# Attention and a multiplicative FFN on one core: the attention part on two 64-row tiles of TensorE instead of one of 128 rows

## The chip, the core and the metric

The kernel runs on one core of a Trainium2 chip. The metric is device time in microseconds (us). In the profile the engines are PE (TensorE matmuls), PEld (its weight loads), DVE (VectorE), ACT (ScalarE), POOL (GpSimd) and SP (which only issues DMAs). Results of TensorE land in PSUM, which the kernel uses as eight banks of 512 float32 columns on 128 partitions.

## What is computed

Attention over 8 batches of 8 heads, with queries pooled in pairs, and then a feed-forward part on the 4608 resulting rows:

```python
# q, k, v: 8 x 8 x 1152 x 64
q_pool = q.reshape(B, H, S // 2, 2, D).mean(axis=3)          # 576 queries per head
scores = scale * np.matmul(q_pool, k.transpose(0, 1, 3, 2))  # 576 x 1152
attn = exp(scores - max) / sum
attn_out = np.matmul(attn, v)
x = attn_out.transpose(0, 2, 1, 3).reshape(4608, 512)
a = x @ w1; b = x @ w2                                       # 512 x 1024 each
h = a * b @ w3                                               # 1024 x 1024
out = h @ w_out                                              # 1024 x 512
```

The kernel multiplies w3 and w_out first (`T16`), so that a row needs w1, w2 and `T16`.

## The kernel before

**Pairs of heads.** Two heads form a pair `p`; there are 32 pairs, four per batch. For each pair k and q come by DMA, POOL casts and pools them into `kq16` (`cast_kq`), and they are transposed into `kqT`: on TensorE for pairs 1 to 7 (`transp_pe`, L323), by DMA from pair 8 on (`transp`). Head 0 of a pair lies on partitions 0 to 63 and head 1 on 64 to 127.

**Slots.** The scores of all pairs are one long strip of columns, cut into 324 slots of 512. A slot (`scores`, L379) is one or two pieces per head, each a matmul of 64 rows; the two heads write two banks of a `psc` buffer, of which there are three. One exponential on ACT (L393) empties a slot into `ring`, which holds 24 x 576 columns, or 2.67 pairs.

**Attention times V.** A pair has five tiles of 128 queries (the last one overlaps, since 576 is not a multiple). A group `av_pair(i)` (L406) is one tile for both heads: 18 matmuls of 128 rows and 65 columns, 64 of V and a constant column that gives the sum. Three column ranges of one bank, `avb`, take turns. DVE takes the reciprocal of the sums and multiplies (`av_norm`, L429); `x_turn` (L443) and `x_copy` (L450) turn the result into `xT`, or from pair 8 on a DMA does (`x_dma`).

**Fill.** The feed-forward part is cut into groups that fill TensorE's time between slots: first the w3 transposes and `T16` (`t_groups`, L467), then for each chunk of 512 rows (`moe_groups`, L522) sixteen projection groups (w1 and w2 in turn, four matmuls of 128 rows and 512 columns each, L506) and four output groups (eight such matmuls, L550). DVE empties a group's bank: a copy `asb` (L535), then a multiplication into `gT` (L539), or a scaled copy `osb` (L560), which is stored. A group's bank is `mo`, of which there is one, or half of a `psc` buffer (`bank`, L462). There are nine chunks. A chunk is handed out when its last attention tile is done, later ones five groups afterwards (`HELD`).

**Order.** The program is written out in visits (from L685). A visit puts out three slots and then a string of pair transposes, attention groups and fill groups that a planner picks:

```python
due = max(due + PACE, plan.t + 2.6)      # PACE = 3.09 for three slots
...
for what in plan.visit(due, ...):        # up to six pieces: P, A, m, s
```

`_Plan` (L122) holds a cost in microseconds for every piece, 0.09 for a change between 64 and 128 rows among them, and the time at which ACT and DVE give each buffer back. `visit` tries the possible strings and takes the cheapest. The planner's times only set the order; on the chip every instruction waits on semaphores for its buffers. After the last slot the rest of the fill runs without attention (the tail): the `psc` buffers take turns there, and ACT takes part of the evacuations.

Of the kernel before, what the change touches and what calls it, by code (L numbers as in the profile page):

```python
# [121 lines left out]
class _Plan:  # L122
# [3 lines left out]
    SWITCH, SLOT, AV, TURN, PAIR, SEEN = 0.09, 0.222, 0.553, 0.055, 0.76, 0.05  # L126
    STEP = {0.5: 0.45, 1: 0.866, 2: 1.73}

    def __init__(self, t):
        self.t = t  # L130
        self.act = self.mo = self.av = self.dve = 0.0
        self.psc = [0.0, 0.0, 0.0]
        self.k = 0
        self.row = True

    def _pe(self, row, free, took):
        if row != self.row:
            self.t += self.SWITCH
            self.row = row
        self.t = max(self.t, free) + took  # L140

    def _psc(self):
        self.k += 1
        return (self.k - 1) % 3

    def scores(self):
        b = self._psc()
        self._pe(True, self.psc[b] + self.SEEN, self.SLOT)
        self.act = max(self.act, self.t + 0.21) + 0.953
        self.psc[b] = self.act + 0.07  # L150

    def fill(self, n, at, scored):
        b = self._psc() if scored else None
        self._pe(False, max(at, (self.psc[b] if scored else self.mo) + self.SEEN), self.STEP[n])
        self.dve = max(self.dve, self.t + 0.2) + 0.69
        if scored:
            self.psc[b] = self.dve + 0.07
        else:
            self.mo = self.dve + 0.07

    def av_group(self, turns):
        self._pe(False, self.av + self.SEEN, self.AV + (self.TURN if turns else 0.0))
        self.dve = max(self.dve, self.t + 0.2) + 0.49 + (0.21 if turns else 0.0)
        self.av = self.dve + 0.02

    def pair(self, at):
        b = self._psc()
        self._pe(False, max(at, self.psc[b] + self.SEEN), self.PAIR)
        self.dve = max(self.dve, self.t + 0.1) + 0.9
        self.psc[b] = self.dve + 0.07  # L170

    def copy(self):
        p = _Plan(self.t)
        p.__dict__.update(self.__dict__)
        p.psc = list(self.psc)
        return p

    def visit(self, due, turns, must, groups, pair_at, eager):


        best = [None, None]

        def end(p, seq, work, av):
            q = p.copy()
            for _ in range(3):
                q.scores()
            lost = q.t - self.t - work - 3 * self.SLOT
            cost = lost + 0.2 * abs(p.t - due) + 0.3 * max(q.av + self.SEEN - q.t, 0.0)
            cost -= eager * min(len(turns), 6) * av
            if best[0] is None or cost < best[0] - 1e-9:  # L190
                best[:] = [cost, seq]

        def step(p, seq, work, av, f, pr):
            if pr == len(pair_at) and av >= must:
                end(p, seq, work, av)
            if len(seq) > 5 or p.t > due + 0.5 and av >= must:
                return
            if pr < len(pair_at):
                q = p.copy()
                q.pair(pair_at[pr])  # L200
                step(q, seq + "P", work + self.PAIR, av, f, pr + 1)
            if av < min(len(turns), 3):
                q = p.copy()
                q.av_group(turns[av])
                step(q, seq + "A", work + self.AV + (self.TURN if turns[av] else 0.0), av + 1, f, pr)
            if f < min(len(groups), 4):
                n, at = groups[f]
                for b in (False, True):
                    q = p.copy()
                    q.fill(n, at, b)  # L210
                    step(q, seq + "ms"[b], work + self.STEP[n], av, f + 1, pr)

        step(self, "", 0.0, 0, 0, 0)
        return best[1]


@with_exitstack
def kernel(
# [53 lines left out]
    avb = ps.tile([128, 512], FP32, tag="av", bufs=1)  # L272
    xpt = avb.bitcast(FP16)[:, 896:1024]
    xps = avb[:, 448:448 + QT]
# [48 lines left out]
    def transp_pe(p):  # L323
        kq16 = pairs[p]
        kqT = att.tile([128, NB, 128], FP16, tag="kqT", bufs=3)
        pt = ps.tile([128, 2, 512], FP32, tag="psc", bufs=3, name="ptk").rearrange("p b c -> p (b c)").bitcast(FP16)
        for n, c in enumerate(range(NB - 1, -1, -1)):
            nc.tensor.transpose(pt[:, c * 128:c * 128 + 128], kq16[:, c].rearrange("p u d -> p (u d)"), ident16)  # L328
        for c0, c1 in ((8, NB), (0, 4), (4, 8)):
            nc.vector.tensor_copy(out=kqT[:, c0:c1].rearrange("p c i -> p (c i)"), in_=pt[:, c0 * 128:c1 * 128])  # L330
        pairs[p] = kq_views(kqT)
# [43 lines left out]
    def turn_bank():  # L375
        return ps.tile([128, 512], FP32, tag="mo", bufs=1, name="ptf").bitcast(FP16)


    def scores(s):  # L379
        psc = ps.tile([128, 2, 512], FP32, tag="psc", bufs=3, name="psc")  # L380
# [25 lines left out]
    def av_pair(i):  # L406
        p, t = i // NT5, i % NT5
        va = vaugs[p % NVA]
        o = (i % 3) * 2 * E1
        for jt in range(NJ):  # L410
            c0 = ((p * NJ + jt) * Sq) % RING + TO[t]
            for u in range(2):
                nc.tensor.matmul(avb[:, o + u * E1:o + u * E1 + E1], ring[:, u, c0:c0 + 128], va[:, u, jt, :],  # L413
                                 start=(jt == 0 and u == 0), stop=(jt == NJ - 1), skip_group_check=True)

    XD = 8
    xb5 = {}

# [7 lines left out]
    def on_pe(i):  # L426
        return i >= 0 and (i // NT5 < XD or i % NT5 == QM)

    def av_norm(i):  # L429
        av = avb[:, (i % 3) * 2 * E1:(i % 3) * 2 * E1 + 2 * E1].rearrange("p (u e) -> p u e", e=E1)  # L430
        nc.vector.reciprocal(out=rzall[:, i, :], in_=av[:, :, D:E1].rearrange("p u o -> p (u o)"))  # L431
        p, t = i // NT5, i % NT5
        if on_pe(i):
            xbt = att.tile([128, 2, D], FP16, tag="xbt", bufs=3)
        else:
            if t == 0:
                xb5[p] = att.tile([128, QM, 2, D], FP16, tag="xb5", bufs=3, name="xb5")
            xbt = xb5[p][:, t]
        nc.vector.tensor_tensor(out=xbt, in0=av[:, :, 0:D],
                                in1=rzall[:, i, :].unsqueeze(2).to_broadcast([128, 2, D]), op=ALU.mult)  # L440
        xbts[i] = xbt

    def x_turn(i):  # L443
        xb = xbts.pop(i).rearrange("p u d -> p (u d)")
        if i % NT5 < QM:
            nc.tensor.transpose(xpt, xb, ident16)
        else:
            nc.tensor.matmul(xps, xb, ident16[:, 128 - QT:128], start=True, stop=True, skip_group_check=True)
# [142 lines left out]
    def fill(scored=False):  # L591
# [7 lines left out]
        if put:  # L599
            put(pt)  # L600
# [196 lines left out]
```

## Time and profile before

| What | Value |
| --- | --- |
| time, median of two runs | 422.69 us (421.59 and 423.79) |
| profiled execution | 421.38 us, its span 419.4 us |
| granted TensorE clock | 1.000 |
| 64-row score matmuls (L388) | 1152, mean 290 ns |
| 128-row attention matmuls (L413) | 2880, mean 193 ns |
| exponentials (L393) | 324, 308.1 us in all, the last one ends at 349.2 us |
| first projection matmul (L506) | starts at 67.2 us |
| HBM read and written | 67.11 and 9.44 MB |

A group's row names line, engine and operation, what is written from what, shapes and count; then its busy time in us, the mean of one in ns, and the idle time of the engine just ahead of it with what ended that. A row of stretches gives, for a window of the span, the busy time and the number of instructions of each engine. A row of the timeline gives start and length in us of instructions that follow one another.

### The profile page before, as it was taken

To read this page: it belongs to the slowest core of one execution; us is meant where nothing else is said; L and a number is where in the kernel's file an instruction comes from. 1 tells how busy PE (TensorE), PEld (TensorE's weight loads), DVE (VectorE), ACT (ScalarE), POOL (GpSimd) and SP (SyncE) were. 2 spreads that over 40 slices of the span, in tenths; PEclk is the share of its full clock that TensorE was granted. 3 is DMA by queue.
4 is the path that set the end of the run, shared out by engine and by line. 5 is a ranking of instruction groups with operands and counts; after the bars stand their busy time and mean duration, and the time that the engine had idled before them with its cause. 6 is when DMAs were issued, how large, how long until landed. Compare 5 with 4: busy or idle time off the path is not lost.

```text
span 419.4 us, 12782 instructions
## 1 busy us (share of the span) xinstructions
PE 406.3 (97%) x5337; PEld 253.2 (60%) x5337; DVE 204.8 (49%) x601; ACT 326.4 (78%) x359; POOL 165.7 (40%) x206
## 2 busy tenths in 40 slices
PE   4899999999999999999999999999999999999995
PEld 2588786566565656665566656666577756444442
DVE  1255666655355545455355534554454546624231
ACT  4888979899899989998899889999899882223231
POOL 5889967360573317250664318340642011000000
PEclk9999999999999999999999999999999999999999
DMA  8999999999798898999979999998896214020203
GB/s 273 265 305 294 287 299 325 279 264 199 188 253 208 234 262 223 272 279 265 251 195 262 253 240 291 209 266 227 225 217 120 56 64 64 14 101 2 100 0 106
DMA packets 90960, 86.34 MB, mean 206 GB/s; under 512 B 59664, under 2 KB 64272, under 8 KB 90896
## 3 DMA queue, kind: packets, MB, share of 16 engines
q1 hardware_dynamic: 81600, 59.32, 58.0%
q0 software_dynamic: 8720, 25.10, 20.6%
q10 hardware_dynamic: 576, 1.05, 0.8%
q8 instruction: 42, 0.69, 0.7%
q14 instruction: 22, 0.18, 0.2%
HBM read 67.11 MB, written 9.44 MB: 183 GB/s over the span
## 4 chain that ended last, share of the span: by engine, by line
PE 94%; ACT 2%; DVE 1%; DMA 1%; issue 1%; POOL 0%; ACTq 0%; POOLq 0%
PE avb L413 22%; PE psc L388 20%; PE mot L506 15%; PE mo L506 15%; PE mo L550 10%; PE mot L550 5%; PE mo L484 3%; ACT ring L393 2%; PE ptk L328 2%; DMA kst<-in_k_dram 1%; PE mot L484 1%; PE mot L475 1%; PE mo L475 1%; DVE kqT L330 1%; PE mol L568 0%
## 5 line engine op out<-in xcount | busy, mean ns | idle before, releaser
L393 ACT ACTIVATE ring<-psc 128x1024 f16<-128x1024 f32 x324 | 308.1, 1025 | 34.4 <-PE psc L388 32.6
L413 PEld LDWEIGHTS <-ring 128*128 128x128 f16 x2880 | 103.6, 98 | 32.1 <-issue 10.4
L413 PE MATMUL avb<-vaug,ring 128*128 128x65 f16 x2880 | 114.4, 193 | 0.1
L388 PE MATMUL psc<-kqT 64*128 64x512 f16 (+7 forms) x1152 | 96.7, 290 | 3.2 <-ACT ring L393 1.0
L388 PEld LDWEIGHTS <-kqT 64*128 64x128 f16 x1152 | 45.6, 95 | 35.0 <-issue 12.3
L300 POOL CAST kq<-kst 128x1152 f16<-128x1152 f32 x31 | 35.7, 1151 | 73.5 <-DMA kqT<-kq 52.6
L431 DVE RECIPROCAL rzall<-avb 128x2 f32<-128x2 f32 x160 | 26.3, 164 | 55.8 <-PE avb L413 26.3
L550 PE MATMUL mo<-T,gT 128*128 128x512 f16 x192 | 45.5, 380 | 0.0
L506 PEld LDWEIGHTS <-w2sb 128*128 128x128 f16 x320 | 28.4, 97 | 26.6 <-issue 2.1
L518 POOL DMA_DIRECT2D out_dram<-osb x21 | 11.7, 555 | 81.0 <-DVE osb L560 45.1
L550 PEld LDWEIGHTS <-gT 128*128 128x128 f16 x280 | 25.5, 98 | 30.1 <-issue 2.9
L506 PEld LDWEIGHTS <-w1sb 128*128 128x128 f16 x320 | 27.9, 97 | 26.0 <-issue 3.6
L313 POOL CAST vaug<-vst 128x1152 f16<-128x1152 f32 x32 | 36.6, 1143 | 8.8 <-DMA vst<-in_v_dram 8.8
L304 POOL TENSOR_TENSOR kq<-qst 128x512 f16<-128x512 f32 x31 | 39.4, 1272 | 1.5 <-DMA qst<-in_q_dram 1.5
L506 PE MATMUL mot<-xT,w2sb 128*128 128x512 f16 x156 | 40.0, 379 | 0.0
L506 PE MATMUL mo<-xT,w1sb 128*128 128x512 f16 (+2 forms) x168 | 39.2, 359 | 0.0
L539 DVE TENSOR_TENSOR gT<-mot,asb 128x512 f16<-128x512 f32 x39 | 26.9, 691 | 23.6 <-PE mot L506 23.6
L535 DVE COPY asb<-mo 128x512 f32<-128x512 f32 x38 | 26.3, 691 | 23.8 <-PE mo L506 23.8
L560 DVE TENSOR_SCALAR osb<-mo 128x512 f32<-128x512 f32 x24 | 16.6, 691 | 39.2 <-PE mo L550 39.2
L533 ACT COPY asb<-mot 128x512 f32<-128x512 f32 x20 | 11.7, 585 | 30.4 <-PE mot L506 30.4
L506 PE MATMUL mot<-xT,w1sb 128*128 128x512 f16 (+2 forms) x152 | 34.9, 356 | 0.0
L506 PE MATMUL mo<-xT,w2sb 128*128 128x512 f16 (+2 forms) x164 | 34.0, 338 | 0.0
(69 smaller groups left out, 275.8 us busy)
## 6 DMA issues: line engine op xcount, KB each, us to landing
vst<-in_v_dram SPq DMA_DIRECT2D x25, 576.0 KB, 4.8
kst<-in_k_dram SPq DMA_DIRECT2D x23, 576.0 KB, 5.7
qst<-in_q_dram SPq DMA_DIRECT2D x23, 512.0 KB, 7.3
out_dram<-osb POOLq DMA_DIRECT2D x21, 256.0 KB, 5.9
kst<-in_k_dram POOLq DMA_DIRECT2D x8, 576.0 KB, 9.5
qst<-in_q_dram POOLq DMA_DIRECT2D x8, 512.0 KB, 10.5
vst<-in_v_dram POOLq DMA_DIRECT2D x7, 576.0 KB, 6.3
out_dram<-osb SPq DMA_DIRECT2D x9, 256.0 KB, 2.0
```

The lines of the kernel that those rows point to most:

```text
L300: nc.gpsimd.tensor_copy(out=kq16[:, 0:NJ].rearrange("p c u d -> p u c d"), in_=kst.rearrange("p u (c d) -> p u c d", d=D))
L304: eng.tensor_tensor(out=kq16[:, NJ:NJ + QM].rearrange("p c u d -> p u c d"), in0=qv[:, :, :, 0], in1=qv[:, :, :, 1], op=ALU.add)
L313: nc.gpsimd.tensor_copy(out=va[:, :, :, 0:D], in_=vs.pop(p).rearrange("p u (c d) -> p u c d", d=D))
L388: nc.tensor.matmul(psc[:, u, f - s * G:f - s * G + ln], kT2[u * 64:u * 64 + 64, jt, :], qpT[u * 64:u * 64 + 64, i0:i0 + ln], start=True, s ...
L393: nc.scalar.activation(out=ring[:, :, r0:r0 + G], in_=psc, func=AF.Exp, bias=0.0, scale=SCALE)
L413: nc.tensor.matmul(avb[:, o + u * E1:o + u * E1 + E1], ring[:, u, c0:c0 + 128], va[:, u, jt, :], start=(jt == 0 and u == 0), stop=(jt == N ...
L431: nc.vector.reciprocal(out=rzall[:, i, :], in_=av[:, :, D:E1].rearrange("p u o -> p (u o)"))
L484: nc.tensor.matmul(pT[:, 0:256], w3T[ft][:, a, :], wosb[:, a, n0:n0 + 256], start=(a == 0), stop=(a == NF - 1))
L506: nc.tensor.matmul(pw[:, d0:d0 + n], wt[:, mc, ft * 128:ft * 128 + 128], xT[:, mc, a:a + n], start=(mc == 0 and d0 == 0), stop=(mc == NC - ...
L535: nc.vector.tensor_copy(out=t["a"], in_=pa)
L539: nc.vector.tensor_tensor(out=t["g"][:, ft, :], in0=pb, in1=t["a"], op=ALU.mult)
L550: nc.tensor.matmul(po, t["g"][:, ft, tt:tt + 128], T16[:, ft, :], start=(ft == 0), stop=(ft == NF - 1))
```

## The change

**All on 64 rows.** Up to the last slot, every product of 128 rows becomes products of 64 rows that come in twos, the one on partitions 0 to 63 and the other on 64 to 127. Scores were that already. A unit (class `Unit`) makes two results at a time, in the two banks of `fb`: for a projection the w1 and the w2 result of one slice, for the output two tiles of 128 rows. In the first half of a unit, rows 0 to 63 add to result 0 and rows 64 to 127 to result 1; in the second half they swap. Between the halves stands a `mark`: a copy by DVE of one element of bank 1, which the second half's first matmul must wait for. A projection unit has two steps of eight matmuls of 64 rows and 512 columns, an output unit or a `T16` unit four. `fb` exists once; a unit's two evacuations on DVE come after its last step.

**Attention times V** is done for two tiles at a time (three groups per pair: tiles 0 and 1, 2 and 3, 4), the two heads in the two banks of `avt`, again in two halves with a mark between. `av_norm` handles both tiles at once. The transposes (`transp_pe`, `x_turn`, w3) are made of 64-row ones likewise.

**Buffers.** `psc` has two buffers of two banks instead of three, `fb` two banks instead of `mo`'s one, `avt` two instead of `avb`'s one.

**Order.** Visits and their search are gone. The program is written out piece by piece: of the pieces whose buffers are free by the plan, a slot goes first, then a pair transpose; of attention and fill, attention if it is behind its slots by more than a pair and else fill; if none is free, the one that will be first. A half does not follow its own first half directly. A slot is held back (`owed`) while the ring has no room. `PACE` is 1.01 per slot, `HELD` is 3. In the tail products are of 128 rows as before; three two-bank buffers take turns.

```diff
-    SWITCH, SLOT, AV, TURN, PAIR, SEEN = 0.09, 0.222, 0.553, 0.055, 0.76, 0.05
-    STEP = {0.5: 0.45, 1: 0.866, 2: 1.73}
+    SLOT, AV, STEP, TURN, KQ, SEEN = 0.226, 0.275, 0.866, 0.06, 0.45, 0.05
...
-    def visit(self, due, turns, must, groups, pair_at, eager):
...
-    avb = ps.tile([128, 512], FP32, tag="av", bufs=1)
+    avt = ps.tile([128, 2, 512], FP32, tag="av", bufs=1)
...
+    ROWS = (slice(0, 64), slice(64, 128))
+
+    def fill_banks():
+        return ps.tile([128, 2, 512], FP32, tag="fb", bufs=1, name="fb")
...
-        psc = ps.tile([128, 2, 512], FP32, tag="psc", bufs=3, name="psc")
+        psc = ps.tile([128, 2, 512], FP32, tag="psc", bufs=2, name="psc")
...
+    def mark(bank, c):
+
+        nc.vector.tensor_copy(out=scrap, in_=bank[0:1, c:c + 1])
+
+    def av_half(i, half):
+        for n, jt, c0, va in av_views(i):
+            for r in (0, 1):
+                u = r ^ half
+                nc.tensor.matmul(avt[:, u, n * E1:n * E1 + E1], ring[ROWS[r], u, c0:c0 + 128], va[ROWS[r], u, jt, :],
+                                 start=(half == 0 and n == 0 and jt == 0), stop=(jt == NJ - 1),
+                                 skip_group_check=True)
+        if not half:
+            mark(avt[:, 1, :], (len(BT[i % NBT]) - 1) * E1)
...
+        def step(self):
+            if self.q == 0:
+                self.pt = fill_banks()
+            if self.single:
+                self.single(self.pt)
+            else:
+                per = self.nk // 4
+                half, k0 = self.q // per, 4 * (self.q % per)
+                for kk in range(k0, k0 + 4):
+                    for r in (0, 1):
+                        j = r ^ half
+                        self.mm(self.pt[:, j, :], j, kk, ROWS[r], half == 0 and kk == 0,
+                                kk == self.nk - 1)
+                if self.q == per - 1:
+                    mark(self.pt[:, 1, :], 0)
+            self.q += 1
+            if self.q == len(self.costs):
+                self.put(self.pt)
...
+            def put(pt):
+                asb = msb.tile([128, CH], FP32, tag="asb", bufs=2, name="asb")
+                nc.vector.tensor_copy(out=asb, in_=pt[:, 0, :])
+                nc.vector.tensor_tensor(out=t["g"][:, ft, :], in0=pt[:, 1, :], in1=asb, op=ALU.mult)
...
-    PACE = 3.09
+    PACE = 1.01
...
+        owed = s < NS and avn[0] < NAB and frees(avn[0]) < s * G + G
...
+        if s < NS and not owed and not (turn_due and s >= turned * FLAT // G):
+            may["S"] = max(plan.scores_at(), due)
+        i = avn[0]
+        if ahalf[0]:
+            if last != "A":
+                may["A"] = swap_at["A"]
+        elif i < NAB and i // NBT in pair_exp and s < NS:
+            may["A"] = max(plan.av + plan.SEEN, pair_exp[i // NBT] + 0.1)
+        if unit:
+            if not (unit.swaps() and last == "F"):
+                may["F"] = swap_at["F"] if unit.swaps() else 0.0
+        elif turn_due:
+            may["P"] = max(plan.fb + plan.SEEN, KQ_AT.get(turned, 0.0))
+        elif head() and s < NS:
+            may["F"] = max(plan.fb + plan.SEEN, head().at)
...
+        now = [w for w in may if may[w] <= plan.t + 0.03]
+        if not now:
+            now = [min(may, key=lambda w: may[w])]
+        if "S" in now:
+            what = "S"
+        elif "P" in now:
+            what = "P"
+        elif "A" in now and "F" in now:
+
+            what = "A" if (i + 3) * FLAT + LAG * G < s * G * NBT else "F"
+        else:
+            what = now[0]
```

## The prediction

> **What bounds the kernel now.** I read the busy table and the chain of waits of the page first, then the costliest groups, then stretches of the span, and last TensorE's own timeline.
>
> ```profile
> PE 406.3 (97%) x5337; PEld 253.2 (60%) x5337; DVE 204.8 (49%) x601; ACT 326.4 (78%) x359; POOL 165.7 (40%) x206
> ...
> PE 94%; ACT 2%; DVE 1%; DMA 1%; issue 1%; POOL 0%; ACTq 0%; POOLq 0%
> ...
> L393 ACT ACTIVATE ring<-psc 128x1024 f16<-128x1024 f32 x324 | 308.1, 1025 | 34.4 <-PE psc L388 32.6
> L413 PE MATMUL avb<-vaug,ring 128*128 128x65 f16 x2880 | 114.4, 193 | 0.1
> L388 PE MATMUL psc<-kqT 64*128 64x512 f16 (+7 forms) x1152 | 96.7, 290 | 3.2 <-ACT ring L393 1.0
> L431 DVE RECIPROCAL rzall<-avb 128x2 f32<-128x2 f32 x160 | 26.3, 164 | 55.8 <-PE avb L413 26.3
> ...
> L539 DVE TENSOR_TENSOR gT<-mot,asb 128x512 f16<-128x512 f32 x39 | 26.9, 691 | 23.6 <-PE mot L506 23.6
> L535 DVE COPY asb<-mo 128x512 f32<-128x512 f32 x38 | 26.3, 691 | 23.8 <-PE mo L506 23.8
> ```
>
> TensorE (PE) ends last: 94% of the chain, and its own groups show almost no idle time. The exponentials (ACT) wait 32.6 us for scores, so ACT has room. The last two rows are the price of emptying a bank, 0.691 us for 512 columns. The stretches say that this holds right through the attention part:
>
> ```profile
> 52.00:134.00 82.00, 81.94 (x1220) 53.02 (x1218) 46.65 (x151) 72.85 (x78) 40.94 (x47) 1.00 0.96 249
> 134.00:216.00 82.00, 81.90 (x1160) 50.16 (x1159) 40.04 (x118) 75.04 (x80) 34.16 (x40) 1.00 0.98 249
> 349.00:419.00 70.00, 65.81 (x409) 31.78 (x405) 29.12 (x64) 16.32 (x33) 0.57 (x1) 1.00 0.18 54
> ```
>
> The columns are PE, PEld, DVE, ACT, POOL, granted clock. PE is full; the clock is 1.00. But busy is not streaming. A matmul's record runs on after its columns have gone in: four matmuls of 512 columns start 216 ns apart and each is shown for 379, so a record ends 163 ns after its stream. PE alone around one visit, and the place where it goes from the fill to the scores:
>
> ```profile
> 150.62 0.81 PE L550 MATMUL mo<-T,gT 128*128 128x512 f16 x3
> 151.27 0.71 PE L413 MATMUL avb<-vaug,ring 128*128 128x65 f16 x18
> 151.91 0.83 PE L388 MATMUL psc<-kqT 64*128 64x512 f16 x10
> 152.67 0.39 PE L550 MATMUL mo<-T,gT 128*128 128x512 f16 x1
> ```
>
> ```profile
> 200.76 0.59 PE L550 MATMUL mo<-T,gT 128*128 128x512 f16 x2
> ...
> 201.29 0.26 PE L388 MATMUL psc<-kqT 64*128 64x192 f16 x2
> ```
>
> In the second fence the last L550 ends at 201.35, so it started at 200.97 and its stream ended at 201.19; the first score matmul, on 64 rows, starts at 201.29: 0.10 us lost. From scores back to 128 rows it is the same. I took every start-to-start of PE in the trace less its columns (N/2.4 ns + 2.5): streams sum to 368.9 us, the rest between the first matmul (4.8) and the last (414.6) is 40.9 us. Of this, 211 changes between 64 and 128 rows take 21.8 (median 0.09 to 0.11), uneven 65-column starts in L413 3.3, the first 30 us 11.2 (4.3 of it changes of rows).
>
> **Part 1: no more changes of rows.** Everything up to the last score is on 64 rows, so about 21 us go. A change from L550 to L413, 128 rows both, shows 0 in 92 cases with a wait, so it is the rows that cost, not the wait.
>
> **Part 2: the streams.** Each 128-row product becomes two 64-row ones that should run side by side. The ten score matmuls above (five pairs, three slots, 1536 columns a member) take 0.83 - 0.17 = 0.66 us, that is 1536/2.4 + 5 x 2.5 ns: a pair costs one. So fill steps stay at 4 x 216 = 0.863 us. For attention-times-V, 65 columns with a new weight load each, the nearest row is a score pair of 64 columns: its second member starts 3 ns after the first, the next pair 28 ns after (median of 34). Ends: 28 ns, and two of today's 30.7 one after the other, 61. I take 30.7 a pair, as the 64-column row is almost this shape: a half of two tiles is 18 pairs, 0.553 us, of one tile 0.277. The transposes halve their columns: w3 64 x 56 ns to 64 pairs of 29, 1.7 us less; kq 98 likewise, 2.6; x turns 0.9. In all 5.2 us less: 363.7.
>
> [...]
>
> **Part 3: one pair of banks for the fill.** Before, a fill group of 0.863 us has bank `mo` or one of the three `psc` buffers, so PE writes the next while DVE empties the last. Now a unit (two results) holds `fb`, the only pair, until both are evacuated: 163 ns to the record's end, 37 to DVE (the trace's usual step), 2 x 0.691 (rows L535, L539, L560), 55 back to PE: **1.67 us** without fill after each unit. Before, nothing of PE waited there, so this is the new term. What can lie in it: score slots of 0.222, at most one per 0.951 us of ACT (308.1/324; `psc` goes from three buffers to two), so about two; and one attention half. Not two: after a first half the `mark` (a 1-element DVE copy, 0.136 by the row of the 1x1 badi, 0.164 at most by the reciprocal) must pass before the second, and DVE, in order, has the unit's 1.38 us ahead of it; if the second half comes in the window, the normalising (0.17 + 0.03 + a 256-element product, between 0.29 and 0.58 by the 0.291 of 128 elements, taken 0.42) also stands behind it, so the next first half waits 2.27 us, longer than fill. Hence halves and fill go in lockstep: first fill half, attention half, second fill half, attention half, wait.
>
> One cycle of a projection unit, by hand: 0.863 + attention half 0.461 (mean of 0.553, 0.553, 0.277) + 0.863 + 1.67, and the slots that come due before the second fill half and must go first (one every 48.2/40.5 = 1.19 us, 1.4 in that time), 0.31: **4.17 us**. The swap of the fill itself (163 + 37 + 136 + 55 = 0.39 us) lies under the attention half and a slot, at no cost; without that cover it would cost 0.39. A unit of two outputs has four steps; there, attention being late, three halves fit in the chain: 3.45 + 1.38 + four slots (4.9 us of chain) 0.92 + 1.67 = **7.42 us**, two attention groups. A batch (576 rows, four head pairs, 12 attention groups, one chunk of 8 + 2 units) then lasts 8 x 4.17 + 2 x 7.42 = **48.2 us**; its PE work is fill 20.7 + attention 20 x 0.553 = 11.1 + 40.5 slots x 0.222 = 9.0, together 40.8. So 7.4 us idle per batch. Attention cannot run ahead of this: scores are held back (`owed`) once the ring is full, 2.67 pairs.
>
> **Part 4: the rest.** Marks: about 160 x 0.14 = 22 us on DVE, which has half its time free; their delay is in the cycles. DMA issues, SP and POOL keep their order; a batch of 48 us instead of about 42.5 asks less of them. Start as now, 11.2 less 4.3 of row changes, 6.9; early w3 units, three windows of 0.7, 2; tail (128 rows, three rotating buffers as today) 0.8.
>
> **The sum.** Chunk 0 can start at about 60 us (67.2 today): 40.5 slots at some 1.05 us, the last three groups in lockstep with w3 units, some 10. The ring lets the last score go once pairs 0 to 29 are done, 90 groups, so 78 are left, 6.5 batches: idle 6.5 x 7.4 = 48. Span: 4.8 + 363.7 + 3.3 + 6.9 + 2 + 0.8 + 48 + 4.8 (last start to end) = 434.3. Cross-check: 60 + 6.5 x 48.2 = 373 for the last score (349 now), then 25 units left, 53.5, six groups 5.5, end 4.8: 437. The mean is 435.7. The profiled execution is 2.0 longer than its span (421.38 to 419.4) and the median of the two runs 1.3 above it, so 439 in the frame of the median; the cycles are taken without the slots that a full ring holds back, worth some 2 us: **437 us**. Its own range: with none or three slots in the chain a cycle is 3.86 to 4.52, over 52 cycles 421 to 455; in the first eight pairs DVE also copies the x turns (0.213 each, two per group), which I leave inside that.
>
> **The rivals.** *The window is covered* (the faster side): if both attention halves and two slots fit in each 1.67 us, 1.67 - 0.92 - 0.44 = 0.31 us stays, times 65 units 20; 386.3 + 20 + 3.3 = **410**. It decides at that one place: under 33/65 = 0.5 us idle per unit the change gains. For it: DVE is half idle and ACT waits for scores. Against: DVE's order, above. *Half covered*: attention gets a second half, 0.46 us, into every other window, 15 us in all: **422**. *Attention pairs don't overlap*: 61 ns a pair, halves doubled; the one in the window is hidden, the others cost 0.46 per projection unit and 1.38 per output unit, 6.5 us per batch, 42 in all: **479**. [...] Against it: the 28 ns row. *The 0.1 us stays* at each change of product because it is not the rows: +21, **458**; the 92 cases with 0 speak against it.
>
> **How the numbers follow.** Forecast 0.50, covered 0.20, half covered 0.16, no overlap 0.10, change cost stays 0.04. About 2% is what a measurement of this kernel can tell from no change: 414.2 and 431.1. Faster takes nearly all of covered and 0.02 of half covered, 0.21; within takes 0.14 of half covered, 0.01 of covered and 0.10 of the forecast's low part, 0.25; slower the rest, 0.54. The range 406 to 456 leaves out 0.08 below and 0.12 above.
>
> **What will show it.** Right: PE has about 65 waits of some 0.7 us before a unit's first fill matmul, released by DVE's second evacuation; projection units start about 4.2 us apart; the last exponential ends near 373 us; ACT's idle time grows; the 0.1 us at changes is gone; a 36-matmul half streams in 0.55 us. Wrong: waits before fill under 0.5 us, attention groups two per unit, the last exponential before 350, or a half of 0.9 us and more.

## The result, and the profile after

The changed kernel takes 475.37 us, the median of two runs (474.31 and 476.43), against 422.69: a ratio of 1.1246, 95% interval 1.108 to 1.1412. It is slower, as forecast. The profiled execution took 474.31 us with a span of 472.5. The forecast of 437 was 38 us short, and its range ended at 456.

The page after: the busy table, TensorE's granted clock by fortieths of the span, the chain of waits, and the groups that answer to those of before (busy time, mean ns of one, idle time just before and what ended most of it).

```profile
PE 404.6 (86%) x8895; PEld 272.1 (58%) x8895; DVE 208.3 (44%) x622; ACT 328.5 (70%) x360; POOL 165.6 (35%) x206
...
PEclk9998989999999999999999999999999999999998
...
PE 63%; ACT 17%; DVE 11%; issue 7%; DMA 1%; ACTq 0%
...
L352 ACT ACTIVATE ring<-psc 128x1024 f16<-128x1024 f32 x324 | 309.6, 1025 | 87.9 <-PE psc L347 86.6
L347 PE MATMUL psc<-kqT 64*128 64x512 f16 (+7 forms) x1152 | 126.9, 294 | 30.2 <-ACT ring L352 18.4
...
L385 PE MATMUL avt<-vaug,ring 64*128 64x65 f16 x5400 | 124.0, 193 | 8.5 <-issue 7.9
L570 PE MATMUL fb<-xT,w1sb 64*128 64x512 f16 (+2 forms) x500 | 112.6, 350 | 11.1 <-DVE gT L577 7.9
...
L576 DVE COPY asb<-fb 128x512 f32<-128x512 f32 x51 | 35.3, 691 | 35.1 <-PE fb L570 35.1
```

TensorE's share of the chain falls from 94% to 63%, and ACT, DVE and "issue" take the rest. No engine does much more work: ACT's exponentials cost what they did (309.6 against 308.1 us), DVE is at 44%. The new thing is waiting. Scores wait 18.4 us for ACT and projections 7.9 us for the second evacuation, where before the scores waited 1.0 us for ACT and projections for nothing, and 7.9 us of the attention matmuls' idle time has no releaser at all ("issue").

Counted from start to start as in the prediction (in the trace of before, products of 512, 256 and 128 columns follow their like 216, 109 and 56 ns apart in the median, so about 0.417 ns a column and 2.5 a matmul), but as a union of streams so that a pair counts once, the streams are now 375.8 us (369.2 by the same count before) and the rest, from the span's start to the last matmul, 91.9 us (45.4). Changes between 64 and 128 rows are 0.7 us of that rest, 19.6 before. What came instead: waits for ACT at a slot 27.5, for a unit's second evacuation 14.7, stops that no semaphore explains 13.4 (15 of them), waits for transposed pairs 10.1, for marks 5.5. (These are gaps of over 0.25 us between streams, not between records, so they are larger than the rows of the page.)

Where in the span, in three stages against the prediction's cross-check:

| stage | predicted | measured |
| --- | --- | --- |
| up to the first projection matmul | 60 | 81.0 |
| from there to the end of the last exponential | 313 | 323.3 |
| from there to the end | 64 | 68.2 |

The stretches of these stages, after (PE, PEld, DVE, ACT, POOL, granted clock, DMA share, GB/s):

```profile
18.00:81.00 63.00, 47.56 (x1271) 34.88 (x1267) 27.28 (x91) 38.48 (x40) 38.34 (x51) 0.92 0.86 250
81.00:143.00 62.00, 53.23 (x1355) 36.78 (x1353) 29.52 (x96) 52.52 (x56) 27.81 (x33) 0.97 0.84 219
143.00:404.00 261.00, 230.50 (x5742) 163.86 (x5735) 122.26 (x371) 208.41 (x219) 86.09 (x99) 1.00 0.76 190
405.00:472.00 67.00, 62.80 (x437) 31.26 (x432) 25.51 (x57) 16.71 (x33) 0.00 (x0) 0.99 0.17 53
```

PE is busy three quarters of the first stage, where before it was full (the stretch from 18 to 68 us had 49.77 of 50 us), and the granted clock is 0.92 there. In the long middle stage the clock is 1.00 and PE is idle 30 of 261 us.

One window between two units, on TensorE, after (start and length in us; in brackets the idle time before and its releaser):

```profile
152.12 0.38 PE L570 MATMUL fb<-xT,w1sb 64*128 64x512 f16 x1
152.28 0.43 PE L347 MATMUL psc<-kqT 64*128 64x384 f16 x4
152.50 0.76 PE L385 MATMUL avt<-vaug,ring 64*128 64x65 f16 x35
153.08 0.35 PE L347 MATMUL psc<-kqT 64*128 64x448 f16 x1
153.10 0.19 PE L385 MATMUL avt<-vaug,ring 64*128 64x65 f16 x1
153.13 0.38 PE L347 MATMUL psc<-kqT 64*128 64x448 f16 x3
153.88 0.39 PE L347 MATMUL psc<-kqT 64*128 64x512 f16 x2 [0.38 <-ACT ring L352]
154.10 0.37 PE L570 MATMUL fb<-xT,w1sb 64*128 64x512 f16 x1
```

The same window on DVE:

```profile
152.53 0.69 DVE L576 COPY asb<-fb 128x512 f32<-128x512 f32 x1 [0.31 <-PE fb L570]
153.25 0.69 DVE L577 TENSOR_TENSOR gT<-fb,asb 128x512 f16<-128x512 f32 x1
153.86 0.14 DVE L379 COPY scrap<-avt 1x1 f32<-1x1 f32 x1
...
156.83 0.69 DVE L576 COPY asb<-fb 128x512 f32<-128x512 f32 x1 [0.22 <-PE fb L570]
```

The unit's stream ends at 152.33 and the next unit starts at 154.10: 1.77 us without fill. In it lie one attention half, two slots, 0.38 us of idle and a third slot. The half's mark, at 153.86, comes behind both evacuations, so no second half could come. Unit follows unit after 4.30 us (152.53 to 156.83; the median over the kernel too). But the idle time stands in front of a slot and is booked on ACT: the written order has the third slot ahead of the fill, and the trace shows them starting in that order, at 153.88 and 154.10.

### The profile page after: what moved, and what is told of

Same layout as the page of the kernel before. It is cut to its first block, busy times and chain, and to the rows that moved or that the text cites. A ratio compares the mean times of both kernels' runs of the same rounds, so it can differ in the third digit from the quotient of the medians.

```text
span 472.5 us, 19961 instructions
## 1 busy us (share of the span) xinstructions
PE 404.6 (86%) x8895; PEld 272.1 (58%) x8895; DVE 208.3 (44%) x622; ACT 328.5 (70%) x360; POOL 165.6 (35%) x206
## 4 chain that ended last, share of the span: by engine, by line
PE 63%; ACT 17%; DVE 11%; issue 7%; DMA 1%; ACTq 0%
PE fb L570 19%; ACT ring L352 17%; PE psc L347 11%; PE avt L385 11%; PE fb L599 8%; PE mot L570 5%; PE fb L529 3%; DVE asb L576 3%; DVE gT L577 3%; PE mot L599 3%; DVE kqT L288 1%; PE avt L394 1%; DVE osb L605 1%; DMA qst<-in_q_dram 1%; DVE T L534 1%
## 5 line engine op out<-in xcount | busy, mean ns | idle before, releaser
L352 ACT ACTIVATE ring<-psc 128x1024 f16<-128x1024 f32 x324 | 309.6, 1025 | 87.9 <-PE psc L347 86.6
L347 PE MATMUL psc<-kqT 64*128 64x512 f16 (+7 forms) x1152 | 126.9, 294 | 30.2 <-ACT ring L352 18.4
L385 PEld LDWEIGHTS <-ring 64*128 64x128 f16 x5400 | 117.6, 96 | 29.5 <-issue 11.6
L385 PE MATMUL avt<-vaug,ring 64*128 64x65 f16 x5400 | 124.0, 193 | 8.5 <-issue 7.9
L570 PE MATMUL fb<-xT,w1sb 64*128 64x512 f16 (+2 forms) x500 | 112.6, 350 | 11.1 <-DVE gT L577 7.9
L570 PE MATMUL fb<-xT,w2sb 64*128 64x512 f16 (+2 forms) x500 | 112.8, 351 | 0.0
L347 PEld LDWEIGHTS <-kqT 64*128 64x128 f16 x1152 | 59.4, 96 | 67.2 <-issue 35.6
L570 PEld LDWEIGHTS <-w2sb 64*128 64x128 f16 (+1 forms) x556 | 47.7, 95 | 30.6 <-issue 10.9
L599 PE MATMUL fb<-T,gT 64*128 64x512 f16 (+1 forms) x416 | 58.4, 376 | 4.9 <-DVE gT L577 2.9
L570 PEld LDWEIGHTS <-w1sb 64*128 64x128 f16 (+1 forms) x556 | 47.7, 95 | 23.5 <-DVE gT L577 3.7
L576 DVE COPY asb<-fb 128x512 f32<-128x512 f32 x51 | 35.3, 691 | 35.1 <-PE fb L570 35.1
L379 DVE COPY scrap<-avt 1x1 f32<-1x1 f32 x90 | 13.0, 144 | 62.9 <-PE avt L385 61.8
L577 DVE TENSOR_TENSOR gT<-fb,asb 128x512 f16<-128x512 f32 x51 | 35.3, 691 | 1.7
L379 DVE COPY scrap<-fb 1x1 f32<-1x1 f32 x67 | 9.8, 147 | 47.8 <-PE fb L570 36.9
```

The source lines that it names most:

```text
L347: nc.tensor.matmul(psc[:, u, f - s * G:f - s * G + ln], kT2[u * 64:u * 64 + 64, jt, :], qpT[u * 64:u * 64 + 64, i0:i0 + ln], start=True, s ...
L352: nc.scalar.activation(out=ring[:, :, r0:r0 + G], in_=psc, func=AF.Exp, bias=0.0, scale=SCALE)
L379: nc.vector.tensor_copy(out=scrap, in_=bank[0:1, c:c + 1])
L385: nc.tensor.matmul(avt[:, u, n * E1:n * E1 + E1], ring[ROWS[r], u, c0:c0 + 128], va[ROWS[r], u, jt, :], start=(half == 0 and n == 0 and jt ...
L570: return [nc.tensor.matmul(o[:, d0:d0 + n], (w1sb, w2sb)[j][rows, kk, ft * 128:ft * 128 + 128], xT[rows, kk, a:a + n], start=start and d0 ...
L576: nc.vector.tensor_copy(out=asb, in_=pt[:, 0, :])
```

## The experiments

Each time is of a single run; the kernel before took 420.8 to 422.5 us beside them. The changed kernel's two runs lie 2.1 us apart, so smaller differences are not read. Some expectations count the first projection by its evacuation, 3 to 6 us after its first matmul; below it is the matmul (81.0 us in the changed kernel). "Stops" are gaps of over 0.25 us behind a stream with no wait recorded on the next matmul. Where an edit changes the order, the kernel also has the two lines on `ahalf` that the third diff shows; they act only when no other piece may be put out.

### How much the window costs

Theory: the window of two evacuations between units sets the middle stage. Rival: ACT does, for which the page books most of the waits.

**One evacuation more.** A third read of the bank goes behind the product; DVE has time for it.

```diff
                 nc.vector.tensor_tensor(out=t["g"][:, ft, :], in0=pt[:, 1, :], in1=asb, op=ALU.mult)
+                nc.vector.tensor_copy(out=asb, in_=pt[:, 0, :])
```

> Each projection unit of the attention part is emptied by three DVE operations (the first copy is made twice), 0.69 us more. Theory 'window': units come 4.98 us apart instead of 4.29, time 475 + 51 x 0.69 = 505 to 512. Rival 'the window is covered by other work and something else bounds': under 485.

It took 507.59 us, 32.2 more, with units 4.93 us apart. In its waits (total, times, longest, all in us but the count) the fill now stands for the new copy:

```profile
ACT ring L352 <- PE psc L347: 118.1, 101, 4.3
...
PE fb L570 <- DVE asb L578: 27.3, 32, 1.5
```

51 units each 0.63 us longer are 32 us. The window is on the path at nearly its full price. ACT is not what bounds: it waits longer for scores than in the changed kernel (118.1 us against 86.6).

**One evacuation less.** The first result isn't read, and the product becomes a scaling of the second.

```diff
-                asb = msb.tile([128, CH], FP32, tag="asb", bufs=2, name="asb")
-                nc.vector.tensor_copy(out=asb, in_=pt[:, 0, :])
-                nc.vector.tensor_tensor(out=t["g"][:, ft, :], in0=pt[:, 1, :], in1=asb, op=ALU.mult)
+                nc.vector.tensor_scalar_mul(out=t["g"][:, ft, :], in0=pt[:, 1, :], scalar1=0.25)
```

> Every projection unit of the attention part is emptied by one DVE operation of 0.69 us instead of two (the w1 result is left out of the product, so the output is not the reference's). Theory 'window' (the single pair of fill banks lets PE idle while DVE empties it): 0.69 us goes from each of some 51 windows, projection units come 3.7 us apart instead of 4.29, time 440 to 455. Rival 'instruction supply' (PE stalls because twice as many instructions must be fetched): units stay about 4.2 us apart, time 468 to 477.

A miss: 461.75 us, only 13.6 less, with the median spacing still 4.30 us (mean 4.13). What TensorE waits for has changed place:

```profile
PE psc L347 <- ACT ring L352: 22.8, 53, 1.0
```

Scores now wait 22.8 us for ACT (18.4 with two evacuations), and none of the larger waits is on the evacuation. So either the window was not what set the time, or the program order, written for evacuations of 1.4 us, kept the old rhythm. To tell these apart the same edit was run with the plan told of it:

```diff
-            unit = Unit(0.0, NC, mm, put, _Plan.STEP, 1.4)
+            unit = Unit(0.0, NC, mm, put, _Plan.STEP, 0.7)
...
+        if not may and ahalf[0]:
+            may["A"] = swap_at["A"]
```

> As e1_one_evac (one DVE operation per projection unit, the w1 result left out of the product), and the plan is told so (0.7 instead of 1.4 us), so that the order follows. Theory 'window, held by the written order' (e1 kept 4.30 us between units because the order puts four slots between them): units now come 3.6 to 3.9 us apart, time 440 to 452. Rival 'something other than the window holds the unit at 4.3' : spacing stays over 4.15, time 458 to 465.

445.93 us, 29.4 less than the changed kernel, with units 3.78 us apart.

```profile
ACT ring L352 <- PE psc L347: 58.4, 65, 4.0
...
PE psc L347 <- ACT ring L352: 9.3, 25, 0.7
```

Only the order differs from the run before it, and it is worth 15.8 us: the slot waits fall from 22.8 to 9.3. So the window of the two evacuations does set the middle stage, and the order holds it in place.

**A single bank for the fill, in the kernel before.** Nothing else of the change is in it: the fill loses its right to the `psc` buffers, and rows of 128, three `psc` buffers and the planner stay.

```diff
-                    for b in (False, True):
+                    for b in (False,):
```

> The kernel before, in visits and in 128-row matmuls, but its planner may put a fill group only into the bank mo, never into a score buffer, until the tail. Theory 'window': a single fill buffer alone costs much of what the change costs: PE must find 0.95 us of other work after each 0.86 us group, it has some 0.9 on average, so 0.1 to 0.3 us idle for each of some 130 groups, time 435 to 460. Rival 'the window only hurts with pairs of results and DVE's marks': 422 to 430.

437.79 us against 420.8, 17 more, and TensorE's idle time by the count above goes from 45.4 to 61.3 us. One result at a time waits for one evacuation of 0.69 us there. A single fill buffer costs even the kernel whose products were left as they were. It shows at the start too: the first projection comes at 77.9 us instead of 67.2, with 65 slots written by then instead of 55. The last exponential ends at 347.7 us, as before (349.2), and the fill that is left over then makes the tail longer.

### Stops without a wait

One of them, on TensorE after:

```profile
40.38 0.70 PE L385 MATMUL avt<-vaug,ring 64*128 64x65 f16 x30
43.31 0.32 PE L385 MATMUL avt<-vaug,ring 64*128 64x65 f16 x6 [2.22 <-issue]
```

In the midst of an attention half, after 30 of its 36 matmuls, nothing starts for over 2 us, and no semaphore is waited for. From 40.90 to 41.86 us an instruction packet of 16 KB was on its way. The page's queue of instructions is longer than before, as is the number of TensorE's instructions, here after:

```profile
q8 instruction: 70, 1.15, 1.0%
```

Before, it was 42 packets and 0.69 MB. TensorE has 17,790 matmuls and loads after and 10,674 before, 254 to a packet both times. Theory: in bursts of short matmuls TensorE uses up its instructions faster than packets come while the data transfers fill the DMA engines. Rival: another buffer's wait that the records don't show.

The trace of the changed kernel decides between the two. Counted over TensorE's matmuls and weight loads, the 15 stops come behind number 703, 959, 1215, 1471 and so on: each count is 191 more than a multiple of 256, without an exception, and 256 is close to the 254 matmuls and loads to a packet. And each stop ends 1.3 to 1.5 us after an instruction packet has landed (the one at 43.31 us, 1.45 after 41.86). A wait for a buffer would not keep to such places, so the stops are instructions that come late. The stops that are left with fewer transfers and with quartered products, below, stand at the same places.

**Fewer transfers.** From pair 4 on, q, k and v are those of an earlier pair and are not loaded.

```diff
...
     def load_kq(p, k_eng, q_eng):
+        if p >= 4:
+            kq[p] = kept["kq", p % 2]
+            return
...
     def load_v(p, eng):
+        if p >= 4:
+            vs[p] = kept["v", p % 2]
+            return
...
```

> From pair 4 on no k, q or v is loaded; the casts read the buffers of pairs 2 and 3 again (output not the reference's). DMA has far less to do, PE's instructions are the same. Theory 'instruction supply, delayed by data DMAs': the 15 stops of PE without a semaphore wait, 13.4 us in all, shrink under 4 us, time 460 to 466. Theory 'window': projection units stay 4.2 to 4.3 us apart, time falls only by what those stops were. Rival 'the fetch is too slow by itself': the stops stay above 10 us.

463.44 us, 11.9 less; four stops of 3.3 us in all instead of fifteen of 13.4. The group of the attention matmuls in its page (eight lines further down than after), where 7.9 us had no releaser:

```profile
L393 PE MATMUL avt<-vaug,ring 64*128 64x65 f16 x5400 | 121.3, 192 | 3.1 <-issue 2.7
```

The instructions are the same, the order is the same, and the stops go with the transfers. In the three kernels with reused loads, this one and two below, the stops come to 2.2 to 6.2 us; in the changed kernel and its variants that keep the loads and the 64-row attention, to 8.9 to 17.9.

**Half the instructions.** Attention with 128-row matmuls, whole, as before; the rest as in the change, and the plan is given the new costs.

```diff
-            av_half(i, ahalf[0])
...
+            av_whole(i)
+            av_end()
...
```

> Attention times V in 128-row matmuls, both halves in one step without a mark, and with changes of rows again; fill and transposes stay in 64-row halves. Halves the instructions of attention (some 2700 matmuls and weight loads less). Theory 'window': the unit's evacuation still stands, but a whole two-tile step (1.1 us) fills more of the window: units 4.0 to 4.4 us apart, one group a unit; time 450 to 472, less than 475 by the stops without a wait (13 us) and the dearer pairs (33 against 30.7 ns, 6 us), more by some 190 row changes of 0.1 us. Theory 'instruction supply': those stops fall under 5 us.

468.56 us. No stop is left, with 6123 matmuls, 49 instruction packets and all the transfers:

```profile
q8 instruction: 49, 0.80, 0.7%
```

Units are 4.63 us apart, outside what was expected: 17.1 us of row changes came back, and the groups are longer. So the 64-row attention by itself costs more in this order than it saves: taking it back gains 6.8 us.

**Many instructions in the kernel before.** Its products of 512 columns are cut into four of 128 (the diff shows the projections; the outputs are cut alike).

```diff
-                nc.tensor.matmul(pw[:, d0:d0 + n], wt[:, mc, ft * 128:ft * 128 + 128], xT[:, mc, a:a + n],
+                for z in range(0, n, 128):
...
+                    nc.tensor.matmul(pw[:, d0 + z:d0 + z + m], wt[:, mc, ft * 128:ft * 128 + 128],
...
```

> The kernel before, with each fill matmul of 512 columns of the projections and outputs made as four of 128 with a weight load each: the streams are 4 x 55.8 = 223 ns instead of 216, about 6 us in all where not hidden, and PE has some 2500 matmuls and weight loads more, 2/3 of the change's increase. Theory 'instruction supply': stops without a wait appear (before has none over 0.25 us), 3 to 10 us, time 430 to 440. Rival 'the supply is no limit by itself, only the bursts of 65-column pairs are': no such stops, time 426 to 430.

428.36 us against 422.51, with two stops of 0.8 us in all.

```profile
PE 412.4 (97%) x7905; PEld 357.4 (84%) x7905; DVE 204.9 (48%) x601; ACT 326.6 (77%) x359; POOL 165.9 (39%) x206
...
q8 instruction: 63, 1.03, 1.0%
```

Nearly as many instructions, 63 packets and the same transfers, and almost no stop. The number alone is not it. What the changed kernel has and this one lacks is bursts of pairs of 65 columns, two matmuls and two loads every 33 ns, where the quarters take some 56 ns for one matmul and one load (an estimate from the transposes of 128 columns in the trace of before, which start 56 ns apart). That it is the pace of the bursts fits both runs, but no run changed the pace alone.

### Why the first projection comes at 81 us

Two of the waits of this stage, on TensorE after:

```profile
64.36 0.22 PE L385 MATMUL avt<-vaug,ring 64*128 64x65 f16 x3 [1.58 <-issue]
...
64.47 0.58 PE L285 MATMUL fb<-ident,kq 64*128 64x64 f16 x28
...
66.69 0.50 PE L347 MATMUL psc<-kqT 64*128 64x256 f16 x6 [1.53 <-DVE kqT L288]
67.03 0.84 PE L515 MATMUL fb<-ident,w3c 64*128 64x64 f16 x32
```

And on DVE, from which the slot at 66.69 waits:

```profile
65.49 1.14 DVE L288 COPY kqT<-fb 128x896 f16<-128x896 f16 x2
```

A pair transpose goes through `fb` too; its two copies take 1.14 us, the next slot needs them, and the w3 transposes need `fb` back. So one chain runs through the one pair of banks: w3 transposes, their copies, two `T16` products with one mark between their halves, their two copies, a pair transpose, its copies. The w3 transposes start at 18.1, 32.9, 51.3 and 67.0 us: 15 to 18 us a round, four rounds, the last product at 77.1.

**Pair transposes earlier**, against the theory that the kqT waits are what delays:

```diff
-        turn_due = turned < NPE and s >= turned * FLAT // G - 2
+        turn_due = turned < NPE and s >= turned * FLAT // G - 6
...
```

> The TensorE transposes of pairs 1 to 7 may be put out six slots ahead of need instead of two. Theory 'pair turns' (the transposes share the only fill banks and the next slot then stands in PE's queue until DVE has copied kqT): the 10 us in which PE waits for kqT fall under 3, the first projection comes 5 to 10 us earlier, time 463 to 470. Theories 'window' and 'instruction supply': no change, 473 to 477, units 4.29 us apart either way.

The kqT waits after 15 us go from 7.9 to 0.5 us, 67 slots are written by the first projection instead of 51, and the time is the same: 474.58 us. The first projection comes later, at 90.8, and the last exponential ends at 404.3 as in the changed kernel. Slots that run ahead only fill the ring; the fill is what the rest waits for. Nor does the later first projection cost anything in the end: the transposes of pairs 6 and 7, which in the changed kernel stand among the first projections (copies at 92.2 and 104.7 us), go ahead of them here, and the second chunk is level again (first product at 143.2 us, 144.7 in the changed kernel). The transposes hold `fb` either way. The theory falls.

**Pair transposes in `psc`**, out of the chain through `fb`, and the plan told so:

```diff
...
-        pt = fill_banks().rearrange("p b c -> p (b c)").bitcast(FP16).rearrange("p (b c) -> p b c", b=2)
+        pt = ps.tile([128, 2, 512], FP32, tag="psc", bufs=2, name="ptk")
...
```

> The TensorE transposes of pairs 1 to 7 go into a score buffer, as before the change, and not into the fill banks; they need not wait for the end of a unit. Theory 'one queue for fb in the first 85 us' (w3 units and pair transposes, each with its evacuation, hold up the slots and so chunk 0): first projection at 66 to 75 us instead of 85, time 455 to 466. Rival 'early loss is instruction supply': first projection stays at 80 or later, time 470 to 476.

A miss: 475.21 us, first projection at 82.3, kqT waits 6.4. With two `psc` buffers the transposes now stand between the slots.

**The plan knows when `kqT` is there**, against the theory that the order is to blame here as in the middle:

```diff
...
-            may["S"] = max(plan.scores_at(), due)
+            may["S"] = max(plan.scores_at(), due, kq_at.get((s * G + G - 1) // FLAT, 0.0))
...
-            plan.fill(may["P"], plan.KQ, 1.0)
+            plan.fill(may["P"], plan.KQ, 1.3)
+            kq_at[turned] = plan.fb + plan.SEEN
```

> The plan holds a pair's first slot back until the transposed keys have been copied (it assumed them there at once), so other work is put in that gap; nothing else changes. Theory 'several small stops': waits for kqT fall from 9.4 us under 4, time 467 to 473. Rival 'order': 474 to 478.

476.37 us, 84.9 for the first projection: no gain. Two combinations with the reused loads asked whether these effects add up. First, early transposes and reused loads:

> Pair transposes up to six slots early (as e2) and no loads from pair 4 on (as e4; output not the reference's). Theory 'the 24 us until chunk 0 add up from several small stops (waits for kqT 6, stops without a wait 8, the lower clock that follows 5)': the first projection comes at 66 to 74 us instead of 81 (e4) or 91 (e2), time 450 to 457. Rival 'the written order itself sets the pace there': first projection at 80 or later, time 461 to 464 as in e4.

461.45 us, against 463.44 with the reused loads alone: no more than those give. The first projection comes at 85.1, later than with the reused loads alone (75.2). Then the plan that knows, and reused loads:

> e9 and e4 together (no loads from pair 4 on; output not the reference's). Theory 'several small stops': first projection at 70 to 77 us, time 453 to 459. Rival 'order': 461 to 464.

461.02 us and 78.8: the same again. The remaining reading was that the chain of work through `fb` is too long, whoever waits in it. Two kernels shorten it by leaving work out.

**Half of `T16`** (the rest is a constant):

```diff
-        for f0 in range(0, NF, 2):
+        for f0 in range(0, NF // 2, 2):
...
+    nc.vector.memset(T16[:, NF // 2:, :], 0.01)
...
```

> Two of the four rounds of w3 transposes and T16 products are left out (that half of T16 is a constant, so the output is not the reference's). It takes 8.8 us of PE work away. Theory 'one chain through fb until chunk 0' (transposes, their evacuation, product, its evacuation, pair transposes, one after the other, some 15 us a round of which 4.4 us is PE work): first projection at 64 to 70 us, time 452 to 462, more than the work that is gone. Rival 'PE work and slot pace until chunk 0': 9 us gained, 465 to 468.

460.96 us, first projection at 69.9. The span is 13.3 us less and the streams are 7.3 us less.

**No transposes on TensorE from pair 2 on** (pairs 2 to 7 use pair 1's k and q):

```diff
     def transp_pe(p):
+        if p >= 2:
+            pairs[p] = pairs[1]
+            return
...
```

> The TensorE transposes of pairs 2 to 7 are left out (these pairs use the keys and queries of pair 1, so the output is not the reference's): 2.5 us of PE work. Theory 'one chain through fb': three of them stand in the chain before chunk 0, each with the wait for the bank, its evacuation and the slot behind it, some 3.5 us: first projection at 70 to 76 us, time 462 to 468. Rival: first projection within 3 us of 84, time 471 to 474.

464.79 us, first projection at 74.7. The span is 9.5 us less and the streams are 4.2 us less, and this although its stops are longer (17.9 us).

Both shorten the span by more than the work that they leave out, by 6.0 and 5.3 us, as the theory of one chain had it.

The granted clock belongs to this too. Its mean of 0.92 is made of stretches at full clock and stretches of 3.41 us at half: in the changed kernel from 33.2, 43.4, 67.3 and 80.9 us, and once at the very end. One of them, with the 3.41 us ahead of it (columns as above):

```profile
63.87:67.28 3.41, 1.39 (x61) 1.14 (x62) 1.92 (x7) 0.21 (x1) 2.16 (x2) 1.00 0.60 237
67.28:70.69 3.41, 3.12 (x84) 2.41 (x77) 1.56 (x5) 3.07 (x4) 3.41 (x6) 0.50 0.12 23
```

PE is busy 1.39 of 3.41 us, and the clock is half in the next 3.41. The starts of these stretches lie whole multiples of 3.41 us apart, and ahead of each of the four PE was busy for 0.35 to 0.43 of the time. No other 3.41 us of that raster between the start (5.8 us) and the tail falls under 0.53, and none of them is followed by half clock. So the half clock came, in this kernel, where stops and waits fell together. At half the clock the four stretches lose at most some 7 us (an estimate from their lengths). With the reused loads one of the four is left; without the pair transposes one as well, from 68.8 us.

Three things delay the first projection, by what their removal gives: half of `T16` 11.1 us, the pair transposes 6.3, the stops 5.2 to 5.8 (half the instructions, fewer transfers). How much of the 21 us each holds is not settled: reused loads also free the DMA engines, each removal also changes the stretches of half clock, and combinations were tried only with edits that gave nothing alone.

No kernel here beats the one before.

## Why the prediction was right in direction and 38 us short

**Part 1, right.** "About 21 us go": row changes fell from 19.6 to 0.7 us, and came back (17.1) when attention alone went to 128 rows. The trace of before prices a change at 0.09 to 0.11 us in the median.

**Part 2, right, one size a little off.** Pairs overlap. A 65-column pair comes every 33 ns in the median where 30.7 was taken, so a half is 0.59 us and not 0.553; over 2700 pairs that is 6 us. The streams are 375.8 against 363.7, and of these 12 us attention makes 8.5 (92.8 us of streams by the same count, 84.3 before).

**Part 3, right.** The window was put at 1.67 us, and the one shown is 1.77; one attention half and not two lies in it, for the reason given (the mark behind 1.38 us of evacuation). Projection units are 4.30 us apart for 4.17, output units 7.5 for 7.42, idle time is 7.0 to 9.3 us a batch for 7.4 from the second chunk on. The slope was tested both ways, +32.2 and (with the order made anew) -29.4 us for 0.69 us of evacuation a unit. From the second chunk on a batch lasts 49 to 53 us for 48.2, with the dearer pairs and 5.4 us of stops in this stage; the first lasts 58. Two pair transposes stand in that one: they go through `fb` between units, which are 7.4 us apart there instead of 4.3. The stage makes 10.3 us of the miss.

**The sum, wrong at its start.** The step that failed is "Chunk 0 can start at about 60 us", and with it "early w3 units, three windows of 0.7, 2" in Part 4. It priced the slots and the last attention groups, and gave the start the idle time of before less the row changes. It left out that w3 units, `T16` units and pair transposes pass one behind the other through the single `fb`: the term of Part 3, not applied to the first 60 us. Measured: 81.0, so 21 of the miss; between 30 and 85 us TensorE is idle for 21 us between streams where 2 were given. A single bank alone puts the first projection of the kernel before off by 10.7 us, and taking work out of the chain brings that of the changed kernel forward by 11.1 and 6.3 us. Even the floor was too low: w2 landed at 64.4 us in this run and at 61.9 before, which the trace of before showed.

**Not foreseen.** The stops, 13.4 us, 8.0 of them before the first projection; the half clock, in four stretches from 33 to 84 us; and the pair transposes' copies (1.14 us each time), which the prediction didn't price, with 7.9 us of waits. The trace of before has almost none of the three. The last stage is 4.2 us longer than forecast: 27 units were left and not 25.

**The sum of the miss** against the cross-check of 437: 21.0 + 10.3 + 4.2 = 35.5, to the span of 472.5.

**The rivals.** *The window is covered* and *half covered* fail by the idle time, 7 us and more in each batch. *Attention pairs don't overlap* (479) came near the time for another reason; a half would stream in over 1 us, and it takes 0.59. *The 0.1 us stays* fails by Part 1.

**What was to show it.** The waits that were to be "released by DVE's second evacuation" are 14.7 us, and 27.5 are booked on ACT, since the written order puts a slot in front of the fill. The spacing was the better sign. The last exponential was to end near 373 and ended at 404.3: it was said only that before 350 would be wrong, and no bound was set on the other side.

## What to carry to other kernels

Price an accumulator that exists once by the record's tail, the hand-over and the whole evacuation, against the work that can be written into that window, and do so in every stage that uses it, the start included. Where a program order is fixed in advance, the wait that the profile names can be the one that the order puts first (here 27.5 us on ACT, at a slot, and 14.7 on the evacuation); shorten the suspected cost with the order made anew (29.4 us here) and not only under the old one (13.6). Before doubling the number of instructions in short matmuls, count the instruction packets (70 here, for 42) and look at how full the DMA engines are (0.86 from 18 to 81 us).

## What the runs showed of the hardware

- TensorE ran out of instructions in the changed kernel. With 8895 matmuls, bursts of 65-column pairs and, up to the first projection, the DMA engines at a share of 0.86, 15 stops cost 13.4 us, each behind an instruction whose count is 191 more than a multiple of 256, and each until 1.3 to 1.5 us after an instruction packet of 16 KB had landed. With most loads gone there were 4 stops and 3.3 us; with 6123 matmuls none; with 7905 longer ones 2 stops and 0.8 us.
- The granted clock fell to half for 3.41 us at a time, each time behind 3.41 us in which PE was busy for 0.35 to 0.43 of the time in the changed kernel; 0.53 and more kept it full there. Two other runs don't keep to these figures: 0.58 lost the clock once (early transposes and reused loads), 0.46 kept it once (one evacuation less). Over a longer stretch the busy share was the same with and without the fall: from 18 to 68 us PE is busy 36.88 of 50 us at 0.92 in the changed kernel and 36.57 at 1.00 without the pair transposes.
- A copy of one element out of PSUM on DVE cost 144 ns (L379 of the changed kernel, the mean over 90), where 512 columns on 128 partitions cost 691 (L576).
